# Top-k attention and two gated layers on one core: the words of the float64 weights are shifted into a PSUM bank, and the first rows of layer 1 get another priority

## The chip, the cores and the metric

The kernel runs on one core of one Trainium2 chip, as one program. The metric is the device time of one execution in microseconds (us). Three runs of the kernel before took 1336.48, 1337.62 and 1339.1 us; the median is 1337.62 us.

## The reference

The inputs are q, k and v of 4 batches, 8 heads, 576 rows and 64 columns, and two sets of weights. Cut to what matters, the reference computes:

```python
scores = (1 / sqrt(64)) * q @ k.T                      # 576 x 576 for each batch and head
kth    = 32nd largest of each row of scores
scores = where(scores >= kth, scores, -1e9)            # top-k mask
attn   = exp(scores - max) ; attn /= sum(attn) + 1e-9
x      = attn @ v                                      # back to 2304 tokens x 512
# layer 1: 512 -> 1536 -> 512
xn = x / sqrt(mean(x * x) + 1e-6) * rms_g
g  = xn @ w_gate ; silu = g / (1 + exp(-g))
y  = (silu * (xn @ w_val)) @ w_out
# layer 2: 512 -> 1536 -> 512, other weights
out = (1 / (1 + exp(-(y @ w_gate2))) * (y @ w_val2)) @ w_out2
```

The six weight matrices arrive as float64; q, k, v and rms_g are float32.

## The kernel before, in words

**Units.** The 2304 tokens are 18 units of 128 rows. Sixteen are full tiles of one batch (`attention_full`, line 680), two are joined from the 64 left-over rows of two batches (`attention_rest`, line 696). A unit of attention is eight passes of `attend` (line 611): TensorE makes 128 x 576 scores in PSUM, VectorE finds the 32 largest of each row by four rounds of MAX8 with three MATCH_REPLACE8 between them and masks the exponentials that ScalarE has made, ScalarE and GpSimd split them in two float16 parts, a transposing DMA turns them, and TensorE multiplies by v. There are 144 passes in all.

**Layers.** Every product of the two layers is made of float16 halves: 12 matmuls where one would do in float32. `gate1` and `out1` (lines 806 and 814) are layer 1 of one unit; `gate2` and `out2` (lines 861 and 871) are layer 2 for a batch of two units. Layer 1's weights stay in SBUF (tiles w1g, w1v, w1o). Layer 2's are written to DRAM as halves and loaded again for every batch (tiles wh when they are made, wl when they are read); the first batch's loads wait for the last piece of them to be written (`load2`, line 852).

**Weights.** Each of the 18 pieces of 512 x 512 weights passes through `prep_piece` (line 419) in four parts of 128 x 512, so there are 72 parts, 36 for layer 1 (`prep1`) and 36 for layer 2 (`prep2`). `load_f32` (line 397) makes float32 out of the float64 bits of a part with integer operations. The part lands in the SBUF tile raw as pairs of 32-bit words, low and high. VectorE shifts the high word left by 3 (TENSOR_SCALAR), then merges the top bits of the same word (SCALAR_TENSOR_TENSOR). The low word's 3 bits are brought in, for every second part, by ScalarE and an addition on GpSimd, and for the other parts by a second SCALAR_TENSOR_TENSOR on VectorE. That makes 72 TENSOR_SCALAR and 108 SCALAR_TENSOR_TENSOR. The result lies in the piece's own tile; a matmul of its squares into the PSUM tile wps finds a scale, and ScalarE and GpSimd then split it into halves in place.

**PSUM.** Eight banks: four for the scores (two tiles sp of two banks), one for pv, and three for everything else: the ring with the tag mm, which serves wps and wmt (weights), kvt, pg, pw, py, yn and po.

**The order of the work.** The kernel is not issued as it is written. `Scheduler.record` collects every operation with a priority (a smaller number goes first) and a planned cost, and `Scheduler.order` (line 212) plays the five engines forward by these costs and writes the order of each engine's queue. On each engine it takes the operation that can start first in the plan and, among those that could start at once, the one with the smallest priority (line 263). An operation that opens a tile can be taken only when the plan has a buffer of its ring free. All of this happens when the program is built; on the chip each queue then runs in order. The planned cost of a VectorE instruction of this kind is (lines 197 and 198):

```python
fast = method in ("tensor_scalar", "tensor_copy", "memset") and not psum
return (8 if method == "reciprocal" else 1) * n / (1.92 if fast else 0.96) + 69 + 60 * min(ptrs, 1), 170
```

**Priorities.** `TAU` is 56 and stands for one unit. Attention of unit n has the priorities 56 n to 56 n + 49 or so, the weights of layer 1 have -28 to 17, those of layer 2 have 44.8 to 53.8. The work of the layers has a position pos, which grows by 56 for each unit's two layers, and the priority (line 957)

```python
E.prio = pos + min(LAG[0] + LAG[1] * pos, LAG[2])
```

with `LAG = (110, 0.5, 160)`; its VectorE instructions get 160 less (`BIAS`). The first batch's layer 1 (units 0 and 1) is pos 0 to 56.

Of the kernel before, what the change touches and what calls it, by code (L numbers as in the profile page):

```python
# [12 lines left out]
I32 = mybir.dt.int32  # L13
U32 = mybir.dt.uint32
AF = mybir.ActivationFunctionType
ALU = mybir.AluOpType
PSUM = bass.MemoryType.PSUM
DRAM = bass.MemoryType.DRAM
P = 128
# [20 lines left out]
PREP1 = (-0.5, 0.1)  # L40
PREP2 = (0.8, 0.02)
LOADS = 0.9
LAG = (110, 0.5, 160)
BIAS = {"vector": 160}


# [277 lines left out]
def topk_attention_moe_kernel(  # L324
# [17 lines left out]
    nc = E = Scheduler(tc)  # L342
# [11 lines left out]
    def pool(name, bufs, **kw):  # L354
        return E.pool(ctx.enter_context(tc.tile_pool(name=name, bufs=bufs, **kw)), bufs, **kw)
# [27 lines left out]
    ps_m = pool("ps_m", 3, space=PSUM)  # L383
# [13 lines left out]
    def load_f32(dst, src, on_pool):  # L397

        if src.dtype == F32:
            nc.sync.dma_start(dst, src)  # L400
            return
        raw = wbig.tile([P, 512, 2], I32, name="raw", tag="w4")
        nc.sync.dma_start(raw.rearrange("p f a -> p (f a)"), src.bitcast(I32))
        lo, hi, d = raw[:, :, 0].bitcast(U32), raw[:, :, 1], dst.bitcast(I32)
        nc.vector.tensor_scalar(d, hi, 3, 0x3FFFFFF8, op0=ALU.logical_shift_left, op1=ALU.bitwise_and)
        nc.vector.scalar_tensor_tensor(
            out=d, in0=hi, scalar=-0x40000000, in1=d, op0=ALU.bitwise_and, op1=ALU.bitwise_or
        )
        if on_pool:

            nc.scalar.activation(raw[:, :, 0], lo, AF.Copy, scale=2.0 ** -29)
            nc.gpsimd.tensor_tensor(out=d, in0=d, in1=raw[:, :, 0], op=ALU.add)
            return
        d = dst.bitcast(U32)
        nc.vector.scalar_tensor_tensor(
            out=d, in0=lo, scalar=29, in1=d, op0=ALU.logical_shift_right, op1=ALU.bitwise_or
        )

    def prep_piece(w, kind, j, g, s, i, place):
# [5 lines left out]
        for c in range(CPJ):  # L425
            r = (c if kind == "in" else j * CPJ + c) * P
            src = w[r : r + P, j * 512 : (j + 1) * 512] if kind == "in" else w[r : r + P, :]
            fs.append(place(c).bitcast(F32))
            load_f32(fs[-1], src, c % 2 == 0)
            if g is None:  # L430

                hb = fs[-1].bitcast(BF16).rearrange("p (f a) -> p f a", a=2)[:, :, 1]
                lhs = [hb[:, f * P : f * P + P] for f in range(CPJ)]
                rhs = lhs
            else:
                sq = wt.tile([P, 512], BF16, name="wsq")
                nc.scalar.activation(sq, fs[-1], AF.Square, scale=g[:, c : c + 1])
                lhs = [ones] * CPJ
                rhs = [sq[:, f * P : f * P + P] for f in range(CPJ)]
            with E.group():  # L440
                for f in range(CPJ):
                    nc.tensor.matmul(
                        ps, lhsT=lhs[f], rhs=rhs[f], start=c + f == 0, stop=c + f == 2 * CPJ - 2
                    )
# [454 lines left out]
    xs, dests, in1, in2, ht1, ht2, w2, acc, state = {}, {}, {}, {}, {}, {}, {}, {}, {}  # L899
# [50 lines left out]
    for b in range(len(batches) + 1):  # L950
# [3 lines left out]
        while any(lists):  # L954
            n = min((n for n in range(2) if lists[n]), key=lambda n: (done[n] + lists[n][0][0] / 2) / total[n])
            cost, f, args = lists[n].pop(0)
            E.prio = pos + min(LAG[0] + LAG[1] * pos, LAG[2])
            f(*args)
# [30 lines left out]
```

## Time and profile before

| | |
|---|---|
| median of the three runs | 1337.62 us |
| time of the profiled execution | 1342.87 us |
| its span, first to last instruction | 1341.1 us |
| mean granted clock of TensorE | 0.966 of full speed |
| busy in the span | TensorE 1104.8, VectorE 1092.0, GpSimd 847.9, ScalarE 811.9 us |

The profile comes from one execution. PE is TensorE (PEld its weight loads), DVE is VectorE, ACT is ScalarE, POOL is GpSimd, SPq the queue of SyncE that issues the DMAs. Nearly every instruction carries the line number 320, since one helper issues them all; so groups are told apart by their tiles (out<-in). Consecutive VectorE instructions are shown overlapping by less than 0.1 us.

### The profile page before, as it was taken

How to read it: one execution, taken by the hardware profiler on the slowest of the kernel's cores; microseconds unless marked ns; L12 is line 12 of the kernel's file. 1: busy time of each engine (PE TensorE's matmuls, PEld its weight loads, DVE VectorE, ACT ScalarE, POOL GpSimd, SP SyncE). 2: the span in 40 equal slices, each digit the busy share in tenths (PEclk: the TensorE clock that was granted, in tenths of full speed). 3: DMA queues.
4: the chain of work that ended last, by engine and by line, in shares of the span. 5: the costliest groups of instructions: out<-in, count | busy, mean ns of one | idle time of the engine just before them, and what ended most of it. 6: DMA issues, size and time to landing. Idle time of an engine off the chain costs nothing.

```text
span 1341.1 us, 41193 instructions
## 1 busy us (share of the span) xinstructions
PE 1104.8 (82%) x16900; PEld 965.3 (72%) x16900; DVE 1092.0 (81%) x2601; ACT 811.9 (61%) x1409; POOL 847.9 (63%) x924
## 2 busy tenths in 40 slices
PE   2223237449899979989999999999999999999998
PEld 1122127338796879779879996996899799799886
DVE  7999999999789688799798999988798798971011
ACT  6756467566566765556676674676776466554421
POOL 4867778887565766557585765767576575745500
PEclk9999998569899989999999999999999999999999
DMA  8663577767569665766876858478676765765243
GB/s 280 185 204 103 159 202 229 216 193 199 119 143 219 137 138 125 177 118 124 182 174 151 193 128 187 112 152 171 175 159 148 184 119 120 158 129 153 96 143 126
DMA packets 321037, 215.55 MB, mean 161 GB/s; under 512 B 278096, under 2 KB 286288, under 8 KB 320848
## 3 DMA queue, kind: packets, MB, share of 16 engines
q1 hardware_dynamic: 320848, 212.92, 65.0%
q8 instruction: 132, 2.16, 0.7%
q14 instruction: 57, 0.47, 0.1%
HBM read 137.37 MB, written 14.16 MB: 113 GB/s over the span
## 4 chain that ended last, share of the span: by engine, by line
PE 41%; DVE 24%; DMA 12%; POOL 9%; issue 6%; ACT 5%; SPq 2%; POOLq 0%; ACTq 0%; DVEq 0%
PE pw L320 13%; PE pg L320 13%; PE po L320 6%; DVE m L320 6%; DMA pt<-ph 6%; DVE w L320 5%; PE py L320 4%; DVE wh L320 4%; POOL ph L320 4%; PE pv L320 3%; POOL sg L320 2%; PE sp L320 2%; DMA qt<-qn 2%; SPq L320 2%; DVE w1v L320 2%
## 5 line engine op out<-in xcount | busy, mean ns | idle before, releaser
L320 DVE MAX8 m<-w 128x8 f32<-128x576 f32 x432 | 317.0, 751 | 2.9
L320 PEld LDWEIGHTS <-wl 128*128 128x128 f16 x5184 | 298.4, 99 | 7.4 <-issue 7.1
L320 POOL TENSOR_TENSOR ph<-e,ph 128x512 f16<-128x512 f32 (+1 forms) x288 | 210.4, 753 | 103.1 <-ACT ph L320 97.6
L320 DVE MATCH_REPLACE8 w<-m,w 128x576 f32<-128x576 f32 x288 | 213.4, 743 | 0.0
L320 ACT ACTIVATE e<-sp,nb,sc 128x576 f32<-128x576 f32 x144 | 118.0, 827 | 104.1 <-DVE w L320 38.9
L320 PE MATMUL pg<-yt,wl 128*128 128x128 f16 x2592 | 160.5, 224 | 5.8 <-ACT yt L320 4.0
L320 PE MATMUL pg<-xt,w1g 128*128 128x128 f16 x2592 | 160.9, 224 | 4.4 <-DMA xt<-sn 3.8
L320 PEld LDWEIGHTS <-w1o 128*128 128x128 f16 (+1 forms) x2640 | 152.2, 99 | 16.6 <-DVE w1o L320 8.5
L320 POOL TENSOR_TENSOR sg<-sg,sv 128x512 f32<-128x512 f32 x102 | 130.7, 1282 | 47.4 <-ACT sv L320 44.2
L320 PEld LDWEIGHTS <-w1g 128*128 128x128 f16 x2592 | 153.7, 101 | 5.3 <-issue 3.1
L320 DVE MAX8 m<-sp 128x8 f32<-128x576 f32 x144 | 108.4, 759 | 57.3 <-PE sp L320 56.3
L320 PE MATMUL pw<-xt,w1v 128*128 128x128 f16 x2592 | 153.7, 219 | 1.0 <-DVE ym L320 0.7
L320 PE MATMUL pw<-yt,wl 128*128 128x128 f16 x2592 | 153.5, 219 | 0.5 <-DVE ym L320 0.5
L320 PE MATMUL py<-ht,w1o 128*128 128x128 f16 x2592 | 149.5, 220 | 0.4 <-ACT sv L320 0.4
L320 PEld LDWEIGHTS <-w1v 128*128 128x128 f16 x2592 | 146.8, 98 | 1.8 <-issue 1.2
L320 POOL TENSOR_TENSOR ht<-sg,ht 128x512 f16<-128x512 f32 x102 | 118.3, 1161 | 44.9 <-ACT ht L320 43.8
L320 ACT ACTIVATE ph<-e 128x576 f16<-128x576 f32 x144 | 97.6, 678 | 79.2 <-DVE e L320 78.5
L320 PE MATMUL po<-wl,ht 128*128 128x512 f16 x648 | 145.2, 379 | 0.0
L320 PE MATMUL sp<-kt,qt 128*128 128x512 f16 (+3 forms) x640 | 99.8, 302 | 41.1 <-DVE e L320 24.6
L320 PE MATMUL pv<-vt,pt 128*128 128x65 f16 (+1 forms) x2240 | 95.4, 199 | 32.8 <-DMA pt<-ph 30.2
L320 DVE SCALAR_TENSOR_TENSOR e<-sp,m,e 128x576 f32<-128x576 f32 x144 | 115.7, 809 | 2.9 <-DVE osc L320 0.3
L320 PEld LDWEIGHTS <-pt 128*128 128x128 f16 (+1 forms) x2240 | 83.8, 104 | 42.3 <-DMA pt<-ph 39.2
(148 smaller groups left out, 1771.8 us busy)
## 6 DMA issues: line engine op xcount, KB each, us to landing
wl<-w2g SPq DMA_DIRECT2D x54, 512.0 KB, 4.8
wl<-w2v SPq DMA_DIRECT2D x54, 512.0 KB, 4.7
wl<-w2o SPq DMA_DIRECT2D x54, 512.0 KB, 4.9
raw<-in_moe_w_gate_dram SPq DMA_DIRECT2D x24, 512.0 KB, 4.6
raw<-in_moe_w_val_dram SPq DMA_DIRECT2D x24, 512.0 KB, 4.5
raw<-in_moe_w_out_dram SPq DMA_DIRECT2D x24, 512.0 KB, 4.6
qr<-in_q_dram SPq DMA_DIRECT2D x32, 128.0 KB, 2.9
kr<-in_k_dram SPq DMA_DIRECT2D x16, 256.0 KB, 3.4
```

What stands on the lines that cost most here:

```text
L320: getattr(eng, method)(*map(real, a), **{n: real(x) for n, x in k.items()})
```

## The change

The first shift of each part goes into a new tile dec of the PSUM ring mm instead of the part's own place in SBUF. The merges read it from there, and the last one writes to SBUF: for the parts that GpSimd finishes, the one merge goes from dec to SBUF; for the others the first merge goes from dec to dec and the second from dec to SBUF. Since the tile is in PSUM, the planned cost of the shift is now the slow line's, 512/0.96 + 69 = 602 ns, where it was 512/1.92 + 69 = 336 ns. The planned cost of a merge is 602 ns in both. The second edit changes `LAG`.

```diff
-LAG = (110, 0.5, 160)
+LAG = (80, 1, 160)
...
-        lo, hi, d = raw[:, :, 0].bitcast(U32), raw[:, :, 1], dst.bitcast(I32)
-        nc.vector.tensor_scalar(d, hi, 3, 0x3FFFFFF8, op0=ALU.logical_shift_left, op1=ALU.bitwise_and)
+        lo, hi, d = raw[:, :, 0], raw[:, :, 1], dst.bitcast(I32)
+
+        t = ps_m.tile([P, 512], I32, name="dec", tag="mm", lane="dec")
+        nc.vector.tensor_scalar(t, hi, 3, 0x3FFFFFF8, op0=ALU.logical_shift_left, op1=ALU.bitwise_and)
+        o = d if on_pool else t
         nc.vector.scalar_tensor_tensor(
-            out=d, in0=hi, scalar=-0x40000000, in1=d, op0=ALU.bitwise_and, op1=ALU.bitwise_or
+            out=o, in0=hi, scalar=-0x40000000, in1=t, op0=ALU.bitwise_and, op1=ALU.bitwise_or
         )
         if on_pool:
 
-            nc.scalar.activation(raw[:, :, 0], lo, AF.Copy, scale=2.0 ** -29)
-            nc.gpsimd.tensor_tensor(out=d, in0=d, in1=raw[:, :, 0], op=ALU.add)
+            nc.scalar.activation(lo, lo.bitcast(U32), AF.Copy, scale=2.0 ** -29)
+            nc.gpsimd.tensor_tensor(out=d, in0=d, in1=lo, op=ALU.add)
             return
-        d = dst.bitcast(U32)
         nc.vector.scalar_tensor_tensor(
-            out=d, in0=lo, scalar=29, in1=d, op0=ALU.logical_shift_right, op1=ALU.bitwise_or
+            out=d.bitcast(U32), in0=lo.bitcast(U32), scalar=29, in1=t.bitcast(U32), op0=ALU.logical_shift_right, op1=ALU.bitwise_or
         )
```

With the new `LAG` the offset added to pos is 80 at the start and grows by 1 per step of pos instead of 0.5, up to the same 160. Layer 1 of unit 0 (pos 0 to 28) moves from the priorities 110 to 124 to 80 to 108, unit 1's (pos 28 to 56) from 124 to 138 to 108 to 136. At pos 60 old and new are equal, between 60 and 100 the new number is up to 10 larger, and from 100 on nothing differs.

## Rows read from the trace of the kernel before

**Rows 1.** The page's 40 equal slices of the span (33.5 us each), busy tenths.

```profile
PE   2223237449899979989999999999999999999998
...
DVE  7999999999789688799798999988798798971011
```

**Rows 2.** Busy time by stretches: PE, PEld, DVE, ACT, POOL, TensorE's clock, DMA share, GB/s.

```profile
20.00:140.00 120.00, 34.01 (x238) 24.10 (x237) 119.17 (x236) 80.10 (x142) 81.98 (x68) 1.00 0.58 173
140.00:300.00 160.00, 74.72 (x830) 60.14 (x830) 157.83 (x333) 97.01 (x168) 132.99 (x117) 0.82 0.71 206
...
320.00:1200.00 880.00, 841.77 (x13558) 746.27 (x13556) 759.41 (x1901) 561.50 (x980) 569.60 (x676) 0.98 0.69 152
...
1222.90:1341.00 118.10, 113.93 (x1618) 96.44 (x1615) 11.61 (x31) 34.92 (x57) 24.63 (x21) 1.00 0.37 124
```

**Rows 3.** The same for instructions of tile raw alone: DVE, ACT, POOL, then as before.

```profile
0.00:300.00 300.00, 167.76 (x180) 22.92 (x36) 51.67 (x36) 0.90 0.67 197
```

**Rows 4.** Timeline of the DMA queue's issues: start, duration, both us.

```profile
300.60 1.31 SPq L320 DMA_TRANSPOSE xt<-sn  x1
302.79 2.59 SPq L320 DMA_DIRECT2D w2o<-wh  x2
305.43 1.50 SPq L320 DMA_DIRECT2D wl<-w2g  x1
```

**Rows 5.** Timeline of TensorE, where layer 2 begins.

```profile
325.85 2.84 PE L320 MATMUL pg<-yt,wl 128*128 128x128 f16 x48
```

**Rows 6.** Groups of VectorE's decoding instructions: busy us, mean ns; idle before.

```profile
L320 DVE SCALAR_TENSOR_TENSOR wh<-raw,wh 128x512 int32<-128x512 int32 (+1 forms) x54 | 51.6, 963 | 0.0
...
L320 DVE TENSOR_SCALAR wh<-raw 128x512 int32<-128x512 int32 x36 | 29.8, 830 | 0.8 <-DMA raw<-in_moe_w_gate_dram 0.8
...
L320 DVE SCALAR_TENSOR_TENSOR w1v<-raw,w1v 128x512 int32<-128x512 int32 (+1 forms) x18 | 20.9, 1172 | 0.0
...
L320 DVE SCALAR_TENSOR_TENSOR w1g<-raw,w1g 128x512 int32<-128x512 int32 (+1 forms) x18 | 19.2, 1077 | 0.1
...
L320 DVE SCALAR_TENSOR_TENSOR w1o<-raw,w1o 128x512 int32<-128x512 int32 (+1 forms) x18 | 18.3, 1022 | 0.0
...
L320 DVE TENSOR_SCALAR w1g<-raw 128x512 int32<-128x512 int32 x12 | 11.3, 944 | 0.1
L320 DVE TENSOR_SCALAR w1v<-raw 128x512 int32<-128x512 int32 x12 | 11.2, 935 | 0.0
...
L320 DVE TENSOR_SCALAR w1o<-raw 128x512 int32<-128x512 int32 x12 | 10.1, 840 | 0.0
```

**Rows 7.** Tile raw: count, duration ns min/median/max, first and last start us, forms.

```profile
L320 DVE SCALAR_TENSOR_TENSOR wh<-raw,wh x54: 666/962/1707, 145.7 to 292.7; 128x512 int32<-128x512 int32 x36, 128x512 uint32<-128x512 uint32 x18
...
L320 DVE TENSOR_SCALAR wh<-raw x36: 402/624/1382, 143.7 to 290.0; 128x512 int32<-128x512 int32 x36
...
L320 POOL TENSOR_TENSOR wh<-wh,raw x18: 1271/1288/1742, 146.4 to 287.7; 128x512 int32<-128x512 int32 x18
```

**Rows 8.** The same of tiles w, e and sg.

```profile
L320 DVE MATCH_REPLACE8 w<-m,w x288: 734/743/752, 30.4 to 1209.0; 128x576 f32<-128x576 f32 x144
...
L320 DVE SCALAR_TENSOR_TENSOR e<-sp,m,e x144: 791/808/821, 50.1 to 1210.7; 128x576 f32<-128x576 f32 x144
...
L320 DVE SCALAR_TENSOR_TENSOR sg<-sg,pw x6: 686/689/689, 1295.0 to 1321.9; 128x512 f32<-128x512 f32 x6
```

**Rows 9.** Stretch 200 to 300, instructions of tile sg alone: DVE, ACT, POOL, as in rows 3.

```profile
200.00:300.00 100.00, 0.00 (x0) 5.58 (x9) 12.12 (x9) 0.71 0.72 213
```

**Rows 10.** Timeline of TensorE, layer 1 of unit 0.

```profile
204.53 4.53 PE L320 MATMUL pg<-xt,w1g 128*128 128x128 f16 x48 [2.35 <-DMA xt<-sn]
...
262.23 10.04 PE L320 MATMUL py<-ht,w1o 128*128 128x128 f16 x144
```

**Rows 11.** Timeline of ScalarE, layer 1 of unit 0.

```profile
209.68 0.68 ACT L320 ACTIVATE g<-pg,c1g 128x512 f32<-128x512 f32 x1
...
279.74 0.69 ACT L320 ACTIVATE sf<-py,ys 128x512 f32<-128x512 f32 x1 [1.74 <-DVE ys L320]
```

## The prediction

> **What bounds the kernel now.** The 40 slices come first, since they show that the span has two halves with different limits [rows 1]: for the first nine or ten slices, to about 320 us, VectorE is full (9 in nearly every slice) and TensorE does little (2 to 4, with single slices of 7); from then on TensorE is at 9 in nearly every slice to the end, and VectorE stops four slices earlier. The stretches put figures on it [rows 2]. From 20 to 140 us VectorE is busy 119.2 of 120 us and TensorE 34.0; from 140 to 300 us VectorE 157.8 of 160 and TensorE 74.7. From 320 to 1200 us TensorE is busy 841.8 of 880 us and VectorE 759.4, and in the last 118.1 us TensorE 113.9. So the first 300 us are VectorE's, and the rest is a queue of TensorE work that starts when VectorE lets it.
>
> The next view is what VectorE does in its 300 us: instructions on the tile raw, that is the decoding of weights, are 167.8 us of them [rows 3]. The others are mostly attention.
>
> The two timelines show what TensorE waits for at the end of that stage [rows 4, 5]. Unit 1's rows are turned at 300.6 us (xt), so its layer 1 can't start before that. The last halves of layer 2's weights are written out at 302.8, the first of them is loaded back at 305.4, and the first product with them is at 325.9. Both gates hang on VectorE: unit 1's attention and the last decoded part pass through it, and it is full.
>
> **The shifts and merges.** The groups give the price now [rows 6]. Shifts: 36 at 830 ns (29.9 us) for layer 2, and 12 each at 944, 935 and 840 ns (32.6) for layer 1; 62.5 us for 72, mean 868 ns. Merges: 54 at 963 ns (52.0) and 18 each at 1172, 1077 and 1022 ns (58.9); 110.9 us for 108, mean 1027 ns.
>
> These means hide a short instruction that often stands. A shift takes 402 ns at best and 1382 at worst, a merge 666 to 1707; the spread, about 1.0 us in both, is under the 1.27 us of GpSimd's addition on the same tiles, which itself goes from 1271 to 1742 [rows 7]. VectorE instructions with one SBUF tensor (MATCH_REPLACE8, 734 to 752 ns) or with one SBUF and one PSUM tensor (the mask, 791 to 821 ns) have no such spread, although the mask runs 144 times across the same GpSimd work [rows 8]. So the standing belongs to the instructions that read two SBUF tensors or run in the shift's fast form, and after the change neither is left: shift SBUF to PSUM, merge SBUF and PSUM to SBUF or PSUM.
>
> What they will cost isn't in the trace for a PSUM destination. The nearest row is a SCALAR_TENSOR_TENSOR of 512 elements with one SBUF and one PSUM operand, 689 ns without spread [rows 8]. I take 689 for both. For merges the ends are 666 (their best in SBUF) and 808 (the mask, with 64 elements more and a scalar from memory): 108 x (1027 - 689) = 36.5 us saved, between 39.0 and 23.7. For shifts the ends are 402 (the fast form kept) and 808: 72 x (868 - 689) = 12.9 us saved, between 33.6 and 4.3. Below nothing lies the case that they still stand, which is a rival below.
>
> The shift is where a rule speaks against the change. Shifts in SBUF take 402 ns where they don't stand [rows 7], 0.29 us under the 689 of the row with a PSUM operand. The Trainium skill ("VectorE: DVE Perf Modes", section "Why PSUM operands drop a tier") says that any PSUM operand caps four-byte data at the single rate. By that rule alone, with no shift ever standing, the shifts would lose 72 x 0.287 = 20.7 us; the row of worst cases says that they stand too often for that, and the mean decides.
>
> Together VectorE gets 49.4 us less to do: 29.5 for layer 1's weights (7.8 from shifts, 21.7 from merges), 19.9 for layer 2's (5.1 and 14.8).
>
> **What of it reaches the end.** In the first stage the next engine is ScalarE, 80.1 us of the 120 [rows 2]; the stage with 29.5 less is about 91 us, where ScalarE is at 88%. I count these 29.5 whole. In the second stage GpSimd is at 133.0 of 160 us [rows 2]; in 140 us it would be at 95%, some of which is its own standing that goes too. An in-order queue so full will hold VectorE up now and then, so I keep 15 of the 19.9. That is 44.4 us: unit 1's rows and the last weights come 44 us earlier, TensorE becomes continuous at about 276 instead of 320, and from there it has the same work. In the long stretch VectorE has room (759.4 of 880), and its attention moves earlier by the same 44 us, so what is late next is nothing new: TensorE's own queue, 95.7% busy.
>
> **The PSUM ring.** dec takes one of three banks for a shift and one or two merges, about 1.4 to 2.1 us a part. wps holds another while a piece is decoded; kvt and layer 1 of unit 0 get the third. While TensorE is at 2 to 4 tenths this costs it nothing; what it can cost VectorE is a rival below. After the last part nothing of it is left.
>
> **The planner.** Its shift becomes 602 ns instead of 336, by the line quoted. For one part (a shift and on average 1.5 merges) it planned 336 + 1.5 x 602 = 1239 ns where the chip took 868 + 1.5 x 1027 = 2409; now it plans 1505 where I expect 1.72 us. The order should fit the chip better. I count nothing; the end is a rival.
>
> **The priority.** It decides only between operations that could start at once. Layer 1 of unit 0 moves in front of the second half of unit 1's attention (priorities 84 to 105) on ScalarE and GpSimd; VectorE has almost nothing of it. In the stage, its three gated products have 12.1 us on GpSimd and 5.6 on ScalarE [rows 9], so unit 1's rows can lose at most about 12 us by it. What they gain nobody waits for: unit 0's out product is done at 272 [rows 10], its rows for layer 2 are scaled from 279.7 on [rows 11], and layer 2 can't start before its weights are back at 305 or later. These operations run between unit 1's already, so I take 0, with 12 as the far end.
>
> **The sum.** 1342.87 - 44.4 = 1298.5 us for an execution like the profiled one. The median of the runs is 5.25 us (0.39%) below that execution, so 1293 us.
>
> **Rivals.**
> *The next engine takes over.* GpSimd, at 95%, keeps the second stage as long as it was, and the earlier layer 1 costs its 12 us on the same engine. Left are 29.5 - 12 = 17.5 us: 1342.87 - 17.5 = 1325.4, about 1320. For it speaks GpSimd's 133 of 160 us, against it that VectorE, not GpSimd, is the full one in every slice.
> *More than the sum.* All 49.4 us arrive and the better order takes half of TensorE's 42 us of idle time after 320 (38.2 + 4.2) [rows 2]: 1342.87 - 70.4 = 1272.5, about 1267. Against it: that idle time comes long after the decoding.
> *The PSUM ring makes it slower.* A product of layer 1 holds its bank from its first matmul to ScalarE's last reading: 5.8 us for a gate (204.5 to 210.4), 18 us for py (262.2 to 280.4) [rows 10, 11]. With wps in the second bank, a dec that the planner has put behind one of these in the third stands until it is read, and VectorE's queue, with everything behind it, stands too. If all six gated products of unit 0 and its py catch a part each, that is 6 x 5.8 + 18 = 53 us, which outweighs the saving from 49 us on; with the 12 us of the priority the end is 1342.87 + 53 + 12 - 49.4 = 1358, about 1353. Against it: the planner opens a dec only where it sees a free bank, and the work is late on the chip by a few us, not each time by a whole hold.
> *It doesn't do what it says.* The wait is tied to reading the raw words beside GpSimd, whatever the other operand; then all of it stays and the shift loses its fast form: 20.7 us more, 1363.6, about 1358. Against it speaks the mask, which reads SBUF and PSUM and never stands [rows 8]. In a sentence of its own: the Trainium skill ("SBUF — State Buffer", section "SBUF: two separate sides") says that GpSimd and VectorE lock a shared pair of ports against each other for a whole instruction, and names for VectorE two SBUF inputs or a two-port mode; by that rule this case is out, and the spread of the merges against the mask agrees.
>
> **Numbers.** My forecast has 0.60, the next engine 0.15, more than the sum 0.10, the ring 0.08, no effect on the wait 0.04; 0.03 is left for an outcome within 0.2%, which is about what a measurement of this kernel tells from none. Faster is 0.60 + 0.15 + 0.10 = 0.85, the same 0.03, slower 0.12. The range runs from 1264, just under the largest gain, to 1326, past the second; left out are the two slow cases and the tails, under 0.2. The unknown price of a shift and merge alone (28 to 73 us off VectorE) stays within it.
>
> **What would show it.** Shifts and merges between 660 and 720 ns with no tail beyond 0.8 us; VectorE's time on raw down from 168 to about 120 us; unit 1's xt at 256 instead of 301 and the last write of w2o at 258; TensorE at 9 from slice 8 or 9 on; the end shifted by the same. Wrong would be: merges that still reach 1.5 us; gaps in VectorE ahead of shifts, released by ScalarE or TensorE (the ring); a VectorE that idles behind GpSimd before 260 us; or the gates early and the end not.

## The result and the profile after

The changed kernel takes 1280.24 us in the median of four runs (1278.71 to 1284.33), the kernel before 1337.49 us; the ratio is 0.9576, with a 95% interval of 0.9549 to 0.9602. That is 57 us less; forecast were 44 (1293 us), and the time lies in the range. The profiled execution took 1278.75 us with a span of 1277.0, 64.1 less than the span before; the profiled execution before (1342.87 us) was slower than all four runs of that kernel, and the one after is among the fastest of its four, so differences between the traces come out some 7 us larger than those between the medians.

The 40 slices of the page, now 31.9 us each [rows 1]:

```profile
PE   2334465568989999999999999999999999999998
...
DVE  6999999998978889997889889897989798880011
ACT  7995766675677666477857656775766475554321
```

TensorE is at 9 from about 320 us on, where it was before. What is new stands ahead of that: 4 to 6 instead of 2 to 4. Stretches of the changed kernel (columns as in [rows 2]):

```profile
20.00:140.00 120.00, 44.86 (x326) 30.42 (x323) 117.93 (x302) 98.44 (x174) 90.03 (x91) 1.00 0.76 220
140.00:300.00 160.00, 102.62 (x1410) 89.49 (x1410) 155.92 (x389) 106.15 (x185) 121.95 (x134) 0.81 0.83 224
...
320.00:1200.00 880.00, 855.80 (x14015) 764.90 (x14012) 726.44 (x1818) 566.05 (x985) 575.47 (x673) 1.00 0.68 153
1200.00:1277.00 77.00, 72.72 (x883) 55.26 (x880) 10.04 (x21) 15.21 (x24) 5.61 (x5) 1.00 0.39 131
```

VectorE is nearly as full as it was up to 300 us (273.9 of the 280 us here, 277.0 before), but less of it is decoding. From 20 to 300 us TensorE does 147.5 us of work instead of 108.7. The rest after 300 us, of the changed kernel:

```profile
300.00:1277.00 977.00, 944.35 (x15143) 835.22 (x15142) 751.40 (x1879) 593.47 (x1030) 594.33 (x690) 1.00 0.66 152
```

and of the kernel before:

```profile
0.00:300.00 300.00, 111.65 (x1084) 86.53 (x1084) 289.10 (x594) 188.60 (x328) 222.25 (x193) 0.90 0.67 197
300.00:1341.00 1041.00, 993.12 (x15816) 878.80 (x15816) 802.91 (x2009) 623.26 (x1082) 625.66 (x731) 0.98 0.66 150
```

TensorE's busy time over the whole span is 1095.8 us by the page after and 1104.8 (111.7 + 993.1) before. So by 300 us the changed kernel has done 1095.8 - 944.4 = 151.4 us of it, 40 more than before; after 300 us it idles 977 - 944.4 = 32.6 us instead of 47.9, 15 less; and the same matmuls are 9 us shorter. 40 + 15 + 9 is the 64 us of the spans. A second profile of the changed kernel has 1101.3 us of TensorE work, so part of the 9 us is a difference between executions and not the change's.

The instructions on raw, stretch 0 to 300, VectorE's time first [rows 3]:

```profile
0.00:300.00 300.00, 116.31 (x180) 23.79 (x36) 46.31 (x36) 0.90 0.80 225
```

Their groups [rows 6]:

```profile
L320 DVE TENSOR_SCALAR dec<-raw 128x512 int32<-128x512 int32 x72 | 48.8, 683 | 3.7 <-DMA raw<-in_moe_w_val_dram 1.8 <-DMA raw<-in_moe_w_out_dram 1.0 <-DMA raw<-in_moe_w_gate_dram 0.7
L320 DVE SCALAR_TENSOR_TENSOR dec<-raw,dec 128x512 int32<-128x512 int32 x36 | 24.6, 683 | 0.0
L320 DVE SCALAR_TENSOR_TENSOR wh<-raw,dec 128x512 int32<-128x512 int32 (+1 forms) x36 | 23.7, 676 | 0.0
```

and durations, min/median/max [rows 7]:

```profile
L320 DVE TENSOR_SCALAR dec<-raw x72: 666/683/696, 9.6 to 265.4; 128x512 int32<-128x512 int32 x72
...
L320 DVE SCALAR_TENSOR_TENSOR dec<-raw,dec x36: 668/683/727, 11.7 to 266.6; 128x512 int32<-128x512 int32 x36
L320 DVE SCALAR_TENSOR_TENSOR wh<-raw,dec x36: 665/676/684, 113.7 to 267.9; 128x512 int32<-128x512 int32 x18, 128x512 uint32<-128x512 uint32 x18
...
L320 POOL TENSOR_TENSOR wh<-wh,raw x18: 1276/1289/1306, 115.7 to 260.9; 128x512 int32<-128x512 int32 x18
```

Nothing stands any more: a shift takes 666 to 696 ns, a merge into PSUM 668 to 727. GpSimd's addition has lost its tail too (1742 before, 1306 now), and its busy time over the span went from 847.9 to 814.0 us.

Whom they stood for can be read instruction by instruction from the trace of the kernel before. Of its 72 shifts, the 24 that start while GpSimd is between two instructions take 395 to 428 ns; the 48 that start while GpSimd is in the middle of one take 1095 ns in the mean. Of the 108 merges, 34 take 666 to 693 ns and 74 take 1187 in the mean, by the same division. Of the 48 shifts 43 end 0.28 us after that GpSimd instruction, to within 20 ns, and 69 of the 74 merges 0.55 us after it. With ScalarE there is no such division: shifts that start beside one of its instructions take 862 ns in the mean, the others 880. One pair of shifts, VectorE and GpSimd of the kernel before:

```profile
68.82 0.41 DVE L320 TENSOR_SCALAR w1v<-raw 128x512 int32<-128x512 int32 x1
69.03 1.34 POOL L320 TENSOR_TENSOR w1v<-w1v,raw 128x512 int32<-128x512 int32 x1 [1.62 <-ACT wsq L320]
69.16 1.50 DVE L320 TENSOR_SCALAR w1o<-raw 128x512 int32<-128x512 int32 x1
```

The first starts while GpSimd is idle. The second starts 0.13 us into GpSimd's addition, which ends at 70.37 us, and ends itself at 70.66. In the changed kernel GpSimd makes no difference: shifts that start beside one of its instructions take 683 ns in the mean, the others 684.

The gates, DMA queue [rows 4]:

```profile
235.62 4.23 SPq L320 DMA_TRANSPOSE xt<-sn  x1
...
277.44 2.58 SPq L320 DMA_DIRECT2D w2o<-wh  x2
280.07 1.26 SPq L320 DMA_DIRECT2D wl<-w2g  x2
```

Unit 1's rows come 62 to 65 us earlier, the last weights only 25.

### The profile page after: what moved, and what is told of

Read it like the earlier page. It is cut to its first block, busy times and chain, and to the rows that moved or that the text cites. A ratio compares the mean times of both kernels' runs of the same rounds, so it can differ in the third digit from the quotient of the medians.

```text
span 1277.0 us, 41198 instructions
## 1 busy us (share of the span) xinstructions
PE 1095.8 (86%) x16900; PEld 958.4 (75%) x16900; DVE 1037.3 (81%) x2601; ACT 811.4 (64%) x1409; POOL 814.0 (64%) x924
## 4 chain that ended last, share of the span: by engine, by line
PE 50%; DMA 10%; DVE 6%; POOL 6%; issue 5%; ACT 4%; SPq 1%; POOLq 0%; ACTq 0%; DVEq 0%
PE pw L320 15%; PE pg L320 14%; PE po L320 8%; DMA pt<-ph 6%; PE py L320 5%; PE pv L320 3%; PE sp L320 3%; DVE m L320 3%; DVE w L320 2%; DMA xt<-sn 2%; POOL ph L320 2%; POOL sg L320 2%; DMA qt<-qn 1%; SPq L320 1%; POOL ht L320 1%
## 5 line engine op out<-in xcount | busy, mean ns | idle before, releaser
L320 PEld LDWEIGHTS <-wl 128*128 128x128 f16 x5184 | 292.5, 98 | 3.9 <-issue 3.7
L320 POOL TENSOR_TENSOR ph<-e,ph 128x512 f16<-128x512 f32 (+1 forms) x288 | 204.5, 735 | 96.3 <-ACT ph L320 93.8
L320 PE MATMUL pg<-yt,wl 128*128 128x128 f16 x2592 | 153.8, 219 | 1.9 <-ACT sv L320 1.8
```

What stands on the lines that cost most here:

```text
L320: getattr(eng, method)(*map(real, a), **{n: real(x) for n, x in k.items()})
```

## The experiments

Ratios are to the kernel before on the same chip; 0.001 is 1.3 us.

**The same order with dec in SBUF.** Every queue holds the same instructions in the same order as in the changed kernel.

```diff
-t.real = t.pool.pool.tile(shape, dtype, name=name, tag=tag, ...)
+src, tag = (self.acc, "acc") if name.startswith("dec") else (t.pool.pool, tag)
+t.real = src.tile(shape, dtype, name=name, tag=tag, ...)
...
+E.acc = mo.pool
```

> The changed kernel with every queue in exactly its order, but the tile dec lies in SBUF (it borrows the two buffers of acc, which nothing uses before layer 2's first output), so only the operands' place differs. Theory A (operands: shifts and merges stand beside GpSimd when both tensors are in SBUF): shifts go back to a mean of about 870 ns and merges to 1030, spread to 1.4 us and more, VectorE's time on raw back from 116 to about 165 us, unit 1's xt and the last w2o write later by 40 to 50 us, time 1320 to 1335 us. Theory B (order: the gain comes from the new order of the queues): shifts and merges may stand, but the time stays within 10 us of the changed kernel's 1280.

It took 1332.35 us, ratio 0.9928 (0.9907 to 0.9948). Groups of this run:

```profile
L320 DVE TENSOR_SCALAR dec<-raw 128x512 int32<-128x512 int32 x72 | 62.7, 875 | 2.7 <-DMA raw<-in_moe_w_out_dram 2.4 <-DMA raw<-in_moe_w_gate_dram 0.2
L320 DVE SCALAR_TENSOR_TENSOR dec<-raw,dec 128x512 int32<-128x512 int32 x36 | 38.5, 1070 | 0.0
L320 DVE SCALAR_TENSOR_TENSOR wh<-raw,dec 128x512 int32<-128x512 int32 (+1 forms) x36 | 34.5, 973 | 0.0
```

and durations, min/median/max:

```profile
L320 DVE TENSOR_SCALAR dec<-raw x72: 402/790/1575, 9.7 to 315.8; 128x512 int32<-128x512 int32 x72
...
L320 DVE SCALAR_TENSOR_TENSOR dec<-raw,dec x36: 674/1006/1742, 11.4 to 317.2; 128x512 int32<-128x512 int32 x36
```

The standing is back with the tile's place alone, shifts with their 402 ns at best among it. All six decoding groups (the three above and the merges into w1g, w1v and w1o) come to 171.2 us here and 121.0 in the changed kernel, 50.2 less. The time differs by 0.9928 - 0.9576 = 0.035, 47 us. Theory A holds, and all but some 3 us of VectorE's saving reaches the end, which is within the intervals of the two ratios. The other 0.0072 (10 us) between this run and the kernel before is the order of the queues.

**Each edit alone.** Decoding through PSUM with the old priority:

```diff
-LAG = (80, 1, 160)
+LAG = (110, 0.5, 160)
```

> The changed kernel with the old LAG (110, 0.5, 160): decoding through PSUM alone. Theory A (operands): shifts 683 and merges 676 ns as in the changed kernel, time 1278 to 1290 us. Theory C (the priority makes the part of the gain beyond the 44 us of the sum): 1290 to 1300 us.

1297.74 us, 0.9663 (0.9628 to 0.9698): 45 us of the 57. The priority without the decoding, in the kernel before:

```diff
-LAG = (110, 0.5, 160)
+LAG = (80, 1, 160)
```

> The kernel before with the new LAG (80, 1, 160) alone, decoding in SBUF. Theory A (operands): VectorE's first stage is as long as before, 1330 to 1345 us. Theory C (priority): 1315 to 1328 us.

1334.09 us, 0.9950 (0.9935 to 0.9965): 7 us. This time is in theory A's range and not in theory C's (1315 to 1328), so alone the priority is worth less than C had it. But I had put it at nothing or a loss, and it gains: 7 us alone and 0.9663 - 0.9576, 12 us, beside the decoding. Theory C is right that it carries what lies beyond the sum.

Where the 7 us arise stays open. TensorE's waits for attention's transposes from 400 to 640 us (total, times, longest) seem to show it, before:

```profile
PE pv L320 <- DMA pt<-ph: 11.6, 9, 4.6
```

and with the new priority alone:

```profile
PE pv L320 <- DMA pt<-ph: 3.8, 7, 1.0
```

But from 320 to 400 us the same wait goes the other way, from 1.2 us before to 7.2 with the new priority. From 320 to 640 us together it is 12.8 and 10.9, so most of the waiting has only moved.

**The planner's figure.** The shift planned at 336 ns again:

```diff
-fast = method in (...) and not psum
+fast = method in (...) and (not psum or n == 512)
```

> The changed kernel, but the planner reckons the shift into PSUM at 336 ns as before instead of 602. Theory A (operands): instruction times as in the changed kernel, 1278 to 1290 us. Theory B (the planner's better figure makes the part of the gain beyond the sum): 1290 to 1305 us, with gaps in VectorE or TensorE before 280 us that the changed kernel hasn't.

1284.15 us, 0.9578 (0.9558 to 0.9598), the same as the changed kernel. Its gates, DMA queue:

```profile
255.81 2.59 SPq L320 DMA_DIRECT2D w2o<-wh  x2
...
264.36 1.30 SPq L320 DMA_TRANSPOSE xt<-sn  x1
```

The weights are done 22 us earlier than in the changed kernel and unit 1's rows 29 us later, and the end is the same. So the planner's figure decides which of the two VectorE does first, and neither gate by itself decides the end.

**Less on GpSimd.** One part in four finished on ScalarE and GpSimd, the others on VectorE:

```diff
-load_f32(fs[-1], src, c % 2 == 0)
+load_f32(fs[-1], src, c == 0)
```

> The changed kernel with one part in four finished on ScalarE and GpSimd instead of one in two: 18 more merges on VectorE (18 x 0.68 = 12 us), 18 conversions less on ScalarE (12 us) and 18 additions less on GpSimd (23 us). Theory A (VectorE's own time sets the first stage): 10 to 14 us slower than the changed kernel, 0.965 to 0.968. Rival (ScalarE, GpSimd and the DMA have become the bound between 20 and 80 us, where ScalarE is busy 57.6 of 60 us): as fast or faster, 0.950 to 0.958.

1296.78 us, 0.9670 (0.9639 to 0.9701). VectorE's time on raw, stretch 0 to 300:

```profile
0.00:300.00 300.00, 129.16 (x198) 12.16 (x18) 23.21 (x18) 0.81 0.73 206
```

12.9 us more on VectorE, 11.6 less on ScalarE and 23.1 less on GpSimd make 0.967 - 0.9576 = 0.0094, 12.6 us more. So VectorE sets the first stage, although from 20 to 80 us in the changed kernel ScalarE is nearly full as well and the DMA share is at 1 (view below). That it comes out us for us is partly luck: the planner makes a new order here too, and the orders tried below differ by as much.

```profile
20.00:80.00 60.00, 21.21 (x134) 14.80 (x132) 58.28 (x147) 57.55 (x105) 50.42 (x47) 1.00 1.00 299
```

**Which half of the priority.** The early half (pos under 60, units 0 and 1 earlier) and the late half (pos 60 to 100 later), each in the changed kernel:

```diff
-E.prio = pos + min(LAG[0] + LAG[1] * pos, LAG[2])
+E.prio = pos + min(80 + pos, 110 + 0.5 * pos, 160)        # early half
+E.prio = pos + min(max(80 + pos, 110 + 0.5 * pos), 160)   # late half
```

> The changed kernel with only the first half of the new priority: the smaller of the old and new number, so units 0 and 1 go earlier (pos under 60) and pos 60 to 100 keeps its old number. Decoding through PSUM with the old priority took 0.9663 of the kernel before, with the new one 0.9576. Theory D (the gain is layer 1 of the first two units done earlier): 0.957 to 0.960. Theory E (it is pos 60 to 100 going later, so that attention isn't held up at 400 to 640 us): 0.964 to 0.968.

> The changed kernel with only the second half of the new priority: the larger of old and new, so pos 60 to 100 goes later and units 0 and 1 keep their old number. Theory D: 0.964 to 0.968. Theory E: 0.957 to 0.960. Theory F (neither half by itself; any reordering moves the time by about 10 us): both halves off both values, or both near one.

The early half took 0.9518 (0.9493 to 0.9543), the late half 0.9671 (0.9650 to 0.9691), that is as if nothing had been done to the priority. The gain is the early half's. Is earlier then better still? LAG (50, 1.5, 160):

> The changed kernel with LAG (50, 1.5, 160): layer 1 of units 0 and 1 earlier by up to 30 more, the rest as late or later. If earlier layer 1 of the first units keeps paying (theory D): 1268 to 1278 us, 0.948 to 0.956. If what was to be had is had: 0.955 to 0.960. If it now holds up unit 1's attention on ScalarE and GpSimd: over 0.962.

0.9709 (0.9650 to 0.9768), 18 us slower than the changed kernel: not monotone, and theory D in its plain form falls. Unit 1's rows come at 248.7 us there, 13 later than in the changed kernel, as the third case has it; on which engine they are held up is not shown. The last four ran on one chip: the changed kernel and the early half again, and the early half starting at 95 and at 65:

```diff
+E.prio = pos + min(95 + 0.75 * pos, 110 + 0.5 * pos, 160)   # start 95
+E.prio = pos + min(65 + 1.25 * pos, 110 + 0.5 * pos, 160)   # start 65
```

> The changed kernel itself, as the common measure for the three runs beside it on this chip: 0.955 to 0.960 of the kernel before, as at first.

> The early half alone (the smaller of old and new number), which took 0.9518 on another chip than the changed kernel's first 0.9576. If it is truly the better one: 0.950 to 0.954 and apart from the changed kernel on this chip. If the difference was the chip's: 0.955 to 0.960 like it.

> The early half with a start of 95, halfway between the old 110 (0.966 to 0.967) and the new 80. Theory D (layer 1 of the first two units earlier pays by itself): between the two, 0.956 to 0.964. Theory F (it is the order that falls out of the planner, gaps in VectorE between 280 and 300 us or none): at either end, 0.950 to 0.955 without the gap or 0.964 to 0.969 with it.

> The early half with a start of 65. Theory D, if earlier keeps paying: 0.944 to 0.951; if it has been had by 80: 0.950 to 0.955. Theory F: anywhere from 0.950 to 0.972, the value going with VectorE's idle time between 200 and 320 us, which was 5 to 8 us in the two fast kernels and 16 to 18 us in the slow ones.

The changed kernel 0.9552 (0.9528 to 0.9576), the early half 0.9552 (0.9519 to 0.9584): the same on one chip, so its first 0.9518 is no gain that repeats, and no version here beats the changed kernel. Start 95: 0.9673 (0.9649 to 0.9696), all of the loss of 110. Start 65: 0.9611 (0.9578 to 0.9644). So 110 and 95 are alike, 80 is 12 to 16 us better, 65 and 50 worse again. That is theory F; it allowed nearly any value for start 65, so what tests it is its measure, VectorE's idle time. With the decoding the same in all, busy times in us:

| kernel | VectorE, 200 to 320 us | VectorE, 0 to 420 us | TensorE, 420 to 460 us | ratio |
|---|---|---|---|---|
| start 110 (decoding alone) | 101.7 | 373.4 | 31.5 | 0.9663 |
| start 50 | 103.3 | 373.6 | 31.9 | 0.9709 |
| start 95, early half | 103.5 | 376.4 | 31.5 | 0.9673 |
| start 110, late half | 104.2 | 376.9 | 30.9 | 0.9671 |
| start 65, early half | 109.6 | 383.3 | 35.5 | 0.9611 |
| start 80, shift planned at 336 ns | 108.9 | 384.1 | 37.8 | 0.9578 |
| start 80 (changed kernel), twice | 113.4, 113.3 | 384.3, 384.1 | 37.5, 37.1 | 0.9576, 0.9552 |
| start 80, early half, twice | 114.5, 114.5 | 385.5, 385.7 | 38.2, 37.9 | 0.9518, 0.9552 |

From 200 to 320 us the measure holds but for one row: with the shift planned at 336 ns VectorE idles 11.1 us, more than with start 65, and the time is the changed kernel's. By 420 us that kernel has caught up, and there all rows fall in line: 384 to 386 us of VectorE work in the faster kernels, 373 to 377 in the four slower ones, and 383 with start 65, which lies between in time too. From the first row to the changed kernel VectorE idles 11.7 us less from 200 to 320 us, and the time is 11.6 us shorter; the two numbers are less exact than they look, since the time's interval alone is some 4 us to each side. The view behind the first row:

```profile
200.00:320.00 120.00, 78.46 (x1074) 68.99 (x1072) 101.69 (x262) 72.04 (x127) 79.13 (x88) 0.76 0.75 202
```

and behind the changed kernel's:

```profile
200.00:320.00 120.00, 79.33 (x1166) 70.13 (x1164) 113.36 (x293) 76.06 (x133) 82.63 (x94) 0.79 0.83 213
```

Most of the idle time is two waits close together. Timeline of VectorE, decoding alone with the old priority:

```profile
289.73 0.15 DVE L320 TENSOR_SCALAR p2t<-qn 128x1 int32<-128x1 int32 x1 [2.64 <-ACT qn L320]
...
298.51 0.22 DVE L320 TENSOR_SCALAR f<-pv,kvs 128x2 f32<-128x2 f32 x1 [7.63 <-PE pv L320]
```

and its DMA queue ahead of them:

```profile
280.47 2.55 SPq L320 DMA_DIRECT2D w2o<-wh  x2
283.82 1.30 SPq L320 DMA_TRANSPOSE qt<-qn  x1
285.21 0.53 SPq L320 DMA_DIRECT2D qr<-in_q_dram  x1
```

In the changed kernel the same two q requests stand ahead of the last weights' write:

```profile
269.32 1.23 SPq L320 DMA_TRANSPOSE qt<-qn  x1
270.65 0.53 SPq L320 DMA_DIRECT2D qr<-in_q_dram  x1
...
277.44 2.58 SPq L320 DMA_DIRECT2D w2o<-wh  x2
```

Without the turned q no new scores can be made; VectorE finishes the passes that it has and then stands for the last one's product (pv). The four slower kernels all have qt at 281 to 287 us, behind the w2o write, and a wait of 6 to 10 us on pv; the changed kernel and the early half starting at 80 have qt at 269 to 271 and no such wait; the one starting at 65 has it at 273.5 and a wait of 4.1. The kernel with the shift planned at 336 ns has qt at 282.3 and a wait of 4.4 on pv as well, and loses nothing by it; there the weights' write was done at 255.8. So a late qt does not decide by itself. That the place of qt is the cause was read from these traces and not tried by moving it alone, and why the planner puts it there for 110, 95 and 50 and not for 80 stays open.

How the idle time reaches the end shows on TensorE. By 320 us it has done as much work with the decoding alone as in the changed kernel (167.8 and 167.3 us). It goes short later, from 420 to 460 us (columns as in [rows 2]), decoding alone:

```profile
420.00:460.00 40.00, 31.53 (x513) 28.85 (x510) 39.57 (x106) 26.62 (x47) 25.85 (x34) 0.87 0.44 80
```

and the changed kernel:

```profile
420.00:460.00 40.00, 37.53 (x678) 35.72 (x675) 36.29 (x97) 29.31 (x53) 27.97 (x32) 1.00 0.63 134
```

With the decoding alone VectorE is full there, and TensorE stands for attention three times in a row:

```profile
433.96 0.59 PE L320 MATMUL pv<-vt,pt 128*128 128x65 f16 x14 [1.99 <-DMA pt<-ph]
437.27 0.95 PE L320 MATMUL pv<-vt,pt 128*128 128x65 f16 x14 [2.71 <-DMA pt<-ph]
441.58 1.12 PE L320 MATMUL sp<-kt,qt 128*128 128x512 f16 x4 [3.35 <-DVE e L320]
```

The other three slower kernels are as short of TensorE work in this stretch, and none of the faster ones is. A VectorE that is some 11 us behind with attention fits these rows; no run tried it alone.

## Why the prediction was right

**The bound.** VectorE's own time sets the first stage: 47 of 50 us reach the end when only the tile's place is changed, and 12.9 us added make 12.6, the latter with a new order that may have moved it as well.

**The price of shifts and merges.** 689 ns were taken for both, 683 and 676 measured, without a tail; 49.4 us less on VectorE were forecast, 50.2 measured at the same order. That the shift would lose its fast form also held, and was outweighed: beside an idle GpSimd a shift in SBUF takes 395 to 428 ns, in PSUM none is under 666. The rival by which the wait stays is refuted by the same rows. The prediction read the wait's length from layer 2's parts alone (shifts to 1382 ns, merges to 1707); over all parts it goes to 1514 and 1846, which changes nothing in its sum, since that goes by the means.

**What of it reaches the end.** 5 us were set aside for GpSimd in the second stage. At the same order about 3 were lost, within the intervals of both ratios, and taking 23.1 us off GpSimd gave nothing back that shows. GpSimd was busy 122 of the 160 us, not 133 of 140: its own standing went as well (33.9 us less over the span), and some of its work came earlier (90.0 us from 20 to 140 instead of 82.0). The sum, 44, stands beside the 45 of the decoding alone partly by luck: in that run VectorE idles 18 us from 200 to 320 us, which neither the kernel before (119.9 of 120 us busy) nor the forecast has.

**The step that was mis-sized is the priority.** It stood in the sum with 0 and a far end of 12 us lost; it gains 12 beside the decoding, 7 alone. The prediction looked at what layer 1's earlier work pushes aside, and whether somebody waits for its product. It left out that a priority moves other operations in every queue of the plan, here a request for q: with the decoding alone it stands behind a write of weights, with the new priority ahead of it. Where it stands behind, VectorE idles, and TensorE goes short some 140 us later; that the one makes the other was read from the traces and not tried. The priority's 12 us are nearly all of the 13 us between the forecast and the result.

**The gates** were forecast together at 256 and 258 us and came at 236 and 277, with TensorE continuous from about 320 as before, not from 276. The planner's dearer shift moved attention ahead of the weights; with the old figure they came at 264 and 256. The time is the same, so the sum over VectorE's work was the right account, and the picture of two gates that move alike was not. The gain came for the most part as 40 us of TensorE work done before 300 us, not as an earlier start of the full stretch.

**The other rivals.** The ring cost nothing that shows: VectorE's waits ahead of a dec, 3.7 us in all, end with DMA loads of raw as far as they are named (3.5), none with ScalarE or TensorE. More than the sum did happen. The 1280 us lie as far from the forecast's 1293 as from the 1267 of that rival, so the size doesn't speak for the one or the other. It came with the priority and not with the planner's better figure, and TensorE's idle time after 300 us fell by 15 us, a third and not half.

## What to carry to other kernels

Read the spread of an instruction's durations before its mean: the same shape at 0.67 and 1.8 us, while others with a PSUM operand never vary, tells of a wait that no semaphore shows; dividing the instructions by what another engine was doing when they started tells whom they wait for; and moving one operand to PSUM took it away even where the best case got slower. Count such a saving whole where the engine is full, and check with the order of the queues held fixed. A priority in a planned order has no local price: it was worth 12 to 16 us at a start of 80, nothing at 95, about half at 65 and nothing at 50. The first things to look at are where the full engine then idles and where the next one goes short of work.

## What the runs showed of the hardware that was not expected

A VectorE instruction on two SBUF tensors, or a shift from SBUF to SBUF, that starts in the middle of a GpSimd instruction nearly always ends a fixed time after it, 0.55 us and 0.28 us (69 of 74 merges, 43 of 48 shifts before). With one of its tensors in PSUM it doesn't stand at all (659 to 727 ns after). GpSimd gains from the other side of the same wait: its 36 subtractions on wh took 1345 ns in the mean before and 1161 now.

TensorE's granted clock over the first 200 us was 0.64 (a mean of its two levels, 1.2 and 2.4 GHz) in one profile of the early half and 0.96 in the other, and TensorE was busy 88.3 and 88.2 us there. From 50 to 100 us it was 0.50 in the one, the lower level, and 1.00 in the other, and the four score matmuls near 66 us took 1.14 us in both. The ends of matmuls are modelled in these traces, so whether the lower clock cost nothing in this stretch of short groups or the times can't show it stays open.
